# Pieces of 256 columns on GpSimd, both low parts on VectorE, and an earlier square, in an attention and mixture-of-experts kernel

## The chip, the core and the metric

The kernel runs on one core of one Trainium2 chip. The metric is device microseconds of one execution; a smaller number is better. The core's engines are TensorE (PE; its weight loads are a row of their own, PEld), VectorE (DVE), ScalarE (ACT), GpSimd (POOL) and SyncE (SP), which issues most of the transfers.

## What is computed

Three layers in float32. First an attention with pooled keys and values: 8 batches, 8 heads, 576 queries, and the keys and values are means over 8 neighbours. Then each of the 4608 tokens goes to the one of 8 experts that it likes best (512 to 1024 to 512). Then a feed-forward layer (512 to 2048 to 512) with a gated activation.

```python
k_p = k.reshape(B, H, Sp, pool, D).mean(axis=3)     # pool = 8, Sp = 72
v_p = v.reshape(B, H, Sp, pool, D).mean(axis=3)
scores = scale * np.matmul(q, k_p.transpose(0, 1, 3, 2))
attn = softmax(scores);  x = attn @ v_p             # then 4608 tokens of 512
logits = normalised(x) @ normalised(expert_emb).T / tau
expert_idx = np.argmax(logits, axis=1)              # one expert for each token
out[mask] = gate_w[mask, None] * (np.maximum(x[mask] @ w1[e], 0.0) @ w2[e])
h = out @ w_in;  g = h * np.clip(h + 3.0, 0.0, 6.0) / 6.0;  return g @ w_out
```

## The kernel before

**Attention.** The 4608 tokens are walked in 36 tiles of 128. Batch b begins at tile 4.5 b. For each tile PE makes the scores (`emit_S`, L434), VectorE takes their maximum and subtracts it (L442, L445), ScalarE takes the exponential (L449), PE transposes (`emit_T`, L455) and multiplies with the pooled values (`emit_P`, L468), and VectorE divides (L476 to L487), two tiles later than the scores. The order of all instructions is written out by hand, each engine works through its own queue in that order, and small steps of the routing (`emit_route`, `emit_pre`, `emit_gate`, `emit_table`) are woven in one by one by `fill`. GpSimd scatters the token numbers to their experts' lists (`scatter`, L127 and L128).

**Pooling.** A sum over 8 is three rounds of adds that halve: 8 to 4, 4 to 2, 2 to 1. For batches 2 to 7 the values are pooled by GpSimd in `pool_v` (L376, L377, L379: one instruction for each round, over 1536, 768 and 384 columns), and the keys by `pool_k0` (L362, two heads on GpSimd and two on VectorE) and then `pool_k` on GpSimd (L367, 576 columns, and L370). Batches 0 and 1 are pooled in smaller parts by `half_v` (L788 to L790) and `head_k` (L795 to L799), shared between the two engines. The pooled keys `kp` and values have two buffers each, the loaded tiles `k_t`, `v_t`, `q_t` too.

**Start.** ScalarE's queue begins with the store of one row of zeros to `x_dram` (L771; it reads a tile that GpSimd clears first) and then the square of the expert embeddings (L774). The square's sum goes through a chain of VectorE steps (`emit_en`: `emit_sqrt`, then L778 to L782), ten of which stand ahead of `head_k` of batch 0 in VectorE's queue.

**Expert blocks.** The tokens are taken in blocks of 256. A block has four steps j; each has its 512 KB of w1 and of w2. Weights are loaded by GpSimd's indirect DMAs (L157) into four buffers, and `emit_wsplit` splits each into a high part (ScalarE, L169) and a low part (one subtraction over 1024 columns, L170); PE multiplies high with high, high with low and low with high (L262 in `emit_h`, L277 in `emit_y`). The low part of w2 is made by VectorE. That of w1 is made by GpSimd in blocks 0 and 1 (`i < KA - 1`) and by VectorE from block 2 on. Three splits ahead of the blocks (in `prep`, behind the last tiles of the attention) are GpSimd's too. `emit_wload` of the weights four steps ahead stands right behind each split, on GpSimd's queue. In the blocks GpSimd also makes the low parts of w_in (L951).

**Last layer.** From about 720 us on, `emit_h3` and `emit_o` (L1087, L1105) run the feed-forward layer in nine groups of 512 tokens.

Of the kernel before, what the change touches and what calls it, by code (L numbers as in the profile page):

```python
# [8 lines left out]
F32 = mybir.dt.float32  # L9
# [5 lines left out]
ALU = mybir.AluOpType  # L15
# [6 lines left out]
def kernel(  # L22
# [13 lines left out]
    nc = tc.nc  # L36
    NB, P, HP, S = q.shape
# [4 lines left out]
    NT, DM = out.shape  # L42
# [3 lines left out]
    NCH = H * SP // CH  # L46
# [10 lines left out]
    KA = 3  # L57
# [18 lines left out]
    XW = DM + GW  # L76
    x_dram = dram.tile([NT + 1, XW], F32, name="x_dram")
# [73 lines left out]
    def emit_wload(nm, g):  # L151
        i, j = divmod(g, NJ)
        if i >= NBLK or ("load", nm, g) in wdone:
            return
        wdone.add(("load", nm, g))

        nc.gpsimd.indirect_dma_start(  # L157
            out=RAW[nm][j], out_offset=None, in_=WROWS[nm],
            in_offset=bass.IndirectOffsetOnAxis(ap=wrow[:, i, j:j + 1], axis=0),
            bounds_check=NROW - 1, oob_is_err=False)  # L160

    def emit_wsplit(nm, g, eng=nc.vector):
        if g >= NJ * NBLK or ("split", nm, g) in wdone:
            return
        wdone.add(("split", nm, g))
        r = RAW[nm][g % NJ]
        h = SPL[nm + "h"]()
        l = SPL[nm + "l"]()
        nc.scalar.activation(out=h, in_=r, func=AF.Copy)  # L169
        eng.tensor_tensor(out=l, in0=r, in1=h.bitcast(F32), op=ALU.subtract)  # L170
        ws[nm, g] = (h, l)
        emit_wload(nm, g + NJ)

# [32 lines left out]
    def emit_gather(i):  # L206
        if i >= NBLK:
            return
        xg_t[i] = []
        for hf in range(2):  # L210
            xg = XG[hf]()
            nc.gpsimd.indirect_dma_start(
                out=xg, out_offset=None, in_=x_dram[0:NPRE_T, :] if i < KA else x_dram,
                in_offset=bass.IndirectOffsetOnAxis(ap=idx_t[i][:, hf, 0:1], axis=0),
            )
            xg_t[i].append(xg)

    def ahead(i):
        emit_regs(i)
        emit_idx(i)  # L220
# [110 lines left out]
    with ExitStack() as p1:  # L331
# [5 lines left out]
        NKP = 2  # L337
        kps = [one.tile([P, HP, 2, SP], F32, name=f"kp{i}") for i in range(NKP)]
# [25 lines left out]
        def pool_k(b, eng):  # L364
            t = k_t.pop(b)
            kp = kps[b % NKP]
            eng.tensor_tensor(out=t[:, :, 0:2, :], in0=t[:, :, 0:2, :], in1=t[:, :, 2:4, :], op=ALU.add)  # L367
            for s in range(2):
                ps = slice(64 * s, 64 * s + 64)
                eng.tensor_tensor(out=kp[ps, :, s, :], in0=t[ps, :, 0, :], in1=t[ps, :, 1, :], op=ALU.add)  # L370
# [2 lines left out]

        def pool_v(b, eng):
            t = v_t.pop(b)
            eng.tensor_tensor(out=t[:, :, 0:4, :], in0=t[:, :, 0:4, :], in1=t[:, :, 4:8, :], op=ALU.add)  # L376
            eng.tensor_tensor(out=t[:, :, 0:2, :], in0=t[:, :, 0:2, :], in1=t[:, :, 2:4, :], op=ALU.add)  # L377
            vs = wk.tile([CH, NCH, D], F32, name="vs")
            eng.tensor_tensor(out=vs, in0=t[:, :, 0, :], in1=t[:, :, 1, :], op=ALU.add)  # L379
            vs_t[b] = vs  # L380

        def head_of(c):
            return 4 * (c // 3) + c % 3
# [330 lines left out]
        def put(n=1):  # L714
            while pend and n > 0:
                n -= 1
                pend.pop(0)()
# [50 lines left out]
            nc.sync.dma_start(out=idx_dram.rearrange("(p a b) o -> p a (b o)", p=P, b=DR),  # L768
                              in_=dummy.unsqueeze(1).to_broadcast([P, IDXN // P // DR, DR * IW]))

        nc.scalar.dma_start(out=x_dram[NT:NT + 1, :], in_=kps[NKP - 1][0:1].rearrange("p h s c -> p (h s c)")[:, 0:XW])  # L771
        esq = xp.tile([P, DM], F32, name="sq")
        ess = one.tile([E, 1], F32, name="ess")
        nc.scalar.activation(out=esq[0:E], in_=emb_sb, func=AF.Square, accum_out=ess)  # L774

        def emit_en():
            rt = yield from emit_sqrt(ess, [E, 1], "e")
            nc.vector.tensor_scalar(out=rt, in0=rt, scalar1=1e-6, scalar2=tau_sb[0:E], op0=ALU.add, op1=ALU.mult)  # L778
            yield
            nc.vector.reciprocal(out=rt, in_=rt)  # L780
            yield
            nc.vector.tensor_scalar(out=emb_sb, in0=emb_sb, scalar1=rt, scalar2=None, op0=ALU.mult)  # L782
            yield

        def half_v(b, g, eng):

            t, o = v_t[b][:, 3 * g:3 * g + 3], vs_t[b][:, 3 * g:3 * g + 3, :]
            eng.tensor_tensor(out=t[:, :, 0:4, :], in0=t[:, :, 0:4, :], in1=t[:, :, 4:8, :], op=ALU.add)  # L788
            eng.tensor_tensor(out=t[:, :, 0:2, :], in0=t[:, :, 0:2, :], in1=t[:, :, 2:4, :], op=ALU.add)
            eng.tensor_tensor(out=o, in0=t[:, :, 0, :], in1=t[:, :, 1, :], op=ALU.add)  # L790

# [161 lines left out]
    def load_y(u, c0=0, c1=KD):  # L953
        nc.sync.dma_start(out=YL[u % 2][:, c0:c1, :].bitcast(F32), in_=yT_dram[:, c0:c1, 512 * u:512 * u + 512])
# [17 lines left out]
    def flush(q_):  # L972
        while q_:
            for g_ in gens + gates:
                g_[1] = False
            fill(100)
# [7 lines left out]
    def block(i, first):  # L984
        key = CONV[i - 1] if 1 <= i <= len(CONV) else None
        for j in range(NJ):
            g = NJ * i + j
            if i == KA - 2 and j == 2:
                flush(gens)
                flush(gates)  # L990
                put(99)
                ahead(KA)
                ahead(KA + 1)
            if j == 0:
                if i >= KA - 1:
                    ahead(i + 3)
                if i == KA - 1:
                    emit_gather(i + 1)
                if i != KA - 2:
                    emit_gather(i + 2)  # L1000
            if j == 0:
                if i == 0:
                    emit_cload(CONV[0])
                if i + 1 < min(NBLK_MIN + 1, len(CONV) + 3):
                    emit_cload((CONV + outs)[i + 1])
            if i == LOADY:
                load_y(0, j, j + 1)
            if i + j:
                emit_h(i, j)
            more()  # L1010
            if key and j:
                (emit_conv_a, emit_conv_b, emit_conv_c)[j - 1](key)
            if j == 2:
                emit_gated(i + 1)
            if j == 3:
                emit_xT(i + 1)
            emit_wsplit("w1", g + 2, nc.gpsimd if i < KA - 1 else nc.vector)
            more()
            if not (first and j == 0):
                emit_y(*divmod(g - 1, NJ))  # L1020
            more()
            if i == 1 and j == 0:
                late_banks()
            if i == 1 and j == 1:
                PHR.append(PHN[0])
            emit_wsplit("w2", g + 1)
            if i == SPLITY:
                split_y(0, j)
# [162 lines left out]
```

## Time and profile before

| | us |
|---|---|
| median of 3 timed runs | 1502.83 (1501.11 to 1508.79) |
| the profiled execution | 1510.78 |
| its span in the trace | 1509.1 |
| PE busy | 1442.2 (96%) |
| PE weight loads busy | 1291.6 (86%) |
| VectorE busy | 786.9 (52%) |
| ScalarE busy | 625.7 (41%) |
| GpSimd busy | 514.2 (34%) |

All times of rows are of the one profiled execution and are counted from its start. A row of a timeline has the start, the duration, the engine, the line, the operation, the tile written and those read, the shapes, and in brackets the idle time before it and what ended it. "x2" on a row means two instructions one after the other, whose time is given together. The column PEclk is the granted clock of TensorE as a share of full speed (2.4 GHz): 0.50 is the lower level, 1.2 GHz.

### The profile page before, as it was taken

What the parts mean: (1) busy time and instruction counts of PE and PEld (TensorE: products, weight loads), DVE (VectorE), ACT (ScalarE), POOL (GpSimd) and SP (SyncE); (2) the same over time, 40 slices, a digit from 0 to 9 for tenths busy, and PEclk for the clock granted to TensorE, in tenths of its full rate; (3) what the DMA queues carried; (4) which work ended last, traced back from release to release, by engine and by line L of the source; (5) the groups of instructions that cost most, each with busy time, mean ns of one, the idle gap of its engine ahead of it and who ended that gap; (6) DMA issues with size and microseconds to landing.
All of it is one profiled execution on the core that took longest, in us unless ns stands there. A gap on an engine that the chain in (4) does not pass through costs nothing.

```text
span 1509.1 us, 22766 instructions
## 1 busy us (share of the span) xinstructions
PE 1442.2 (96%) x8874; PEld 1291.6 (86%) x8874; DVE 786.9 (52%) x1261; ACT 625.7 (41%) x986; POOL 514.2 (34%) x518
## 2 busy tenths in 40 slices
PE   4997887999999999999999999999999999999997
PEld 4987777999999999999878888888888888888885
DVE  6887747777776777665785322223232322323221
ACT  2663653565565656554443322222222222223221
POOL 6576587755656556554222010010101000010101
PEclk9997998999999999999999999999999999999998
DMA  9875531745742263252321010000101000000000
GB/s 287 289 253 169 156 128 30 245 129 165 242 145 74 58 202 98 59 157 46 127 85 57 0 57 0 29 29 1 56 0 58 1 29 29 27 31 1 28 0 28
DMA packets 88451, 136.15 MB, mean 90 GB/s; under 512 B 43369, under 2 KB 58409, under 8 KB 85874
## 3 DMA queue, kind: packets, MB, share of 16 engines
q1 hardware_dynamic: 45024, 69.10, 14.4%
q0 software_dynamic: 33488, 55.80, 12.2%
q10 hardware_dynamic: 9826, 9.74, 2.0%
q8 instruction: 72, 1.18, 0.3%
q14 instruction: 41, 0.34, 0.1%
HBM read 161.51 MB, written 33.33 MB: 129 GB/s over the span
## 4 chain that ended last, share of the span: by engine, by line
issue 38%; PE 7%; DVE 3%; POOL 2%; ACT 1%; POOLq 0%; ACTq 0%; DVEq 0%
POOL out_dram L128 2%; PE ph L1087 2%; PE psx L1105 2%; PE psz L1105 2%; PE psy L1087 2%; DVE cva L939 1%; DVE rg L1091 1%; DVE cva L941 1%; DVE gl L1094 1%; ACT gh L1093 1%; DVE cva L940 0%; DVE yl L959 0%; POOL apart L127 0%; DVE cva L942 0%; POOL wol L951 0%
## 5 line engine op out<-in xcount | busy, mean ns | idle before, releaser
L157 POOL DMA_INDIRECT rw<-in_w_dram,wrow x179 | 214.1, 1196 | 177.0 <-DVE w1l L170 125.5
L128 POOL DMA_INDIRECT out_dram<-os,idc x36 | 35.1, 975 | 657.7 <-ACT os L1115 651.3
L1091 DVE SCALAR_TENSOR_TENSOR rg<-rg,ph 128x512 f32<-128x512 f32 x72 | 49.6, 689 | 206.3 <-ACT rg L1090 206.3
L1094 DVE TENSOR_TENSOR gl<-rg,gh 128x512 fp32r<-128x512 f32 x144 | 99.8, 693 | 100.7 <-ACT gh L1093 100.0
L1093 ACT ACTIVATE gh<-rg 128x512 fp32r<-128x512 f32 x144 | 91.2, 633 | 145.8 <-DVE rg L1091 141.5
L1091 DVE SCALAR_TENSOR_TENSOR rg<-rg,psy 128x512 f32<-128x512 f32 x72 | 49.5, 687 | 178.5 <-ACT rg L1090 178.5
L1090 ACT ACTIVATE rg<-ph,half 128x512 f32<-128x512 f32 x72 | 49.4, 686 | 208.1 <-PE ph L1087 200.9
L1090 ACT ACTIVATE rg<-psy,half 128x512 f32<-128x512 f32 x72 | 49.4, 686 | 198.7 <-PE psy L1087 198.7
L277 PE MATMUL psy<-hh,w2h 128*128 128x256 f32 x640 | 129.5, 283 | 0.0
L277 PE MATMUL psy<-hl,w2h 128*128 128x256 f32 x640 | 127.6, 281 | 0.0
L277 PE MATMUL psy<-hh,w2l 128*128 128x256 f32 x640 | 127.6, 280 | 0.0
L170 DVE TENSOR_TENSOR w2l<-rw,w2h 128x1024 fp32r<-128x1024 f32 x84 | 110.3, 1313 | 20.8 <-ACT w2h L169 17.6
L170 DVE TENSOR_TENSOR w1l<-rw,w1h 128x1024 fp32r<-128x1024 f32 x76 | 102.7, 1351 | 26.4 <-ACT w1h L169 13.9
L1105 PE MATMUL psx<-wol,gh 128*128 128x512 f32 x288 | 112.4, 390 | 0.4 <-POOL wol L951 0.4
L1105 PE MATMUL psx<-woh,gh 128*128 128x512 f32 x288 | 112.1, 389 | 0.0
L1105 PE MATMUL psx<-woh,gl 128*128 128x512 f32 x288 | 112.0, 389 | 0.0
L1105 PE MATMUL psz<-woh,gh 128*128 128x512 f32 x288 | 112.0, 389 | 0.0
L1105 PE MATMUL psz<-woh,gl 128*128 128x512 f32 x288 | 112.0, 389 | 0.0
L1105 PE MATMUL psz<-wol,gh 128*128 128x512 f32 x288 | 112.0, 389 | 0.0
L265 ACT ACTIVATE hh<-ph 128x512 fp32r<-128x512 f32 x78 | 46.6, 598 | 146.7 <-PE ph L262 131.2
L169 ACT ACTIVATE w2h<-rw 128x1024 fp32r<-128x1024 f32 x85 | 89.9, 1057 | 31.3 <-PE psy L277 20.6
L262 PE MATMUL ph<-xh,w1l 128*128 128x256 f32 x624 | 98.7, 280 | 3.4 <-POOL w1l L170 3.4
(235 smaller groups left out, 3327.5 us busy)
## 6 DMA issues: line engine op xcount, KB each, us to landing
yT_dram<-ys SPq DMA_DIRECT2D x21, 512.0 KB
x_dram<-x ACTq DMA_DIRECT2D x36, 256.0 KB
raw<-in_w_in_dram SPq DMA_DIRECT2D x16, 512.0 KB
raw<-in_w_out_dram SPq DMA_DIRECT2D x16, 512.0 KB
yl<-yT_dram SPq DMA_DIRECT2D x8, 1024.0 KB
k_t<-in_k_dram SPq DMA_DIRECT2D x7, 1152.0 KB
q_t<-in_q_dram SPq DMA_DIRECT2D x7, 1152.0 KB
v_t<-in_v_dram SPq DMA_DIRECT2D x7, 1152.0 KB
```

The lines of the kernel that those rows point to most:

```text
L128: ins = nc.gpsimd.indirect_dma_start(out=dst, out_offset=bass.IndirectOffsetOnAxis(ap=idx, axis=0), in_=src, in_offset=None)
L157: nc.gpsimd.indirect_dma_start(out=RAW[nm][j], out_offset=None, in_=WROWS[nm], in_offset=bass.IndirectOffsetOnAxis(ap=wrow[:, i, j:j + 1], ...
L169: nc.scalar.activation(out=h, in_=r, func=AF.Copy)
L170: eng.tensor_tensor(out=l, in0=r, in1=h.bitcast(F32), op=ALU.subtract)
L262: nc.tensor.matmul(ph[:, f, :], lhsT=a[:, c, fs], rhs=b[:, c, :], start=(n == 0), stop=(n == 3 * KD - 1))
L277: nc.tensor.matmul(o, lhsT=a[:, f, P * c:P * c + P], rhs=b[:, f, :], start=(j == 0 and n == 0 and c % 2 == 0), stop=(j == NJ - 1 and n == ...
L1087: nc.tensor.matmul(ph, lhsT=a[:, c, :], rhs=b[:, c, :], start=(n == 0), stop=(n == 3 * KD - 1))
L1090: nc.scalar.activation(out=r, in_=ph, func=AF.Relu, scale=1.0 / 6.0, bias=half)
L1091: nc.vector.scalar_tensor_tensor(out=r, in0=r, scalar=1.0, in1=ph, op0=ALU.min, op1=ALU.mult)
L1093: nc.scalar.activation(out=gh, in_=r, func=AF.Copy)
L1094: nc.vector.tensor_tensor(out=gl, in0=r, in1=gh.bitcast(F32), op=ALU.subtract)
L1105: nc.tensor.matmul(PO[a], lhsT=x[:, ts], rhs=w, start=(f == 0 and n == 0), stop=(f == NF - 1 and n == 2))
```

## The change

Four edits. (1) In `pool_k`, `pool_v` and the first round of `half_v`, an add is cut along its columns into pieces of 256 (or 288, 192) columns; the same columns are added. (2) In `emit_wsplit`, where GpSimd makes the low part, it does so in four pieces of 256 columns; VectorE still takes 1024 at once. (3) In the blocks 0 and 1, the low part of w1 is no longer given to GpSimd: VectorE makes it, as in the later blocks. (4) ScalarE's queue begins with the square of the embeddings, and the zero row's store follows it. The tile `vs` in `pool_v` is taken ahead of the adds.

```diff
@@ emit_wsplit
-        eng.tensor_tensor(out=l, in0=r, in1=h.bitcast(F32), op=ALU.subtract)
+        n = 256 if eng is nc.gpsimd else 1024
+        for c in range(0, 1024, n):
+            eng.tensor_tensor(out=l[:, c:c + n], in0=r[:, c:c + n], in1=h[:, c:c + n].bitcast(F32), op=ALU.subtract)
@@ pool_k
-            eng.tensor_tensor(out=t[:, :, 0:2, :], in0=t[:, :, 0:2, :], in1=t[:, :, 2:4, :], op=ALU.add)
+            for h in range(0, HP, 2):
+                eng.tensor_tensor(out=t[:, h:h + 2, 0:2, :], in0=t[:, h:h + 2, 0:2, :], in1=t[:, h:h + 2, 2:4, :], op=ALU.add)
@@ pool_v
-            eng.tensor_tensor(out=t[:, :, 0:4, :], in0=t[:, :, 0:4, :], in1=t[:, :, 4:8, :], op=ALU.add)
-            eng.tensor_tensor(out=t[:, :, 0:2, :], in0=t[:, :, 0:2, :], in1=t[:, :, 2:4, :], op=ALU.add)
             vs = wk.tile([CH, NCH, D], F32, name="vs")
-            eng.tensor_tensor(out=vs, in0=t[:, :, 0, :], in1=t[:, :, 1, :], op=ALU.add)
             vs_t[b] = vs
+            for c in range(NCH):
+                eng.tensor_tensor(out=t[:, c, 0:4, :], in0=t[:, c, 0:4, :], in1=t[:, c, 4:8, :], op=ALU.add)
+            for c in range(0, NCH, 2):
+                eng.tensor_tensor(out=t[:, c:c + 2, 0:2, :], in0=t[:, c:c + 2, 0:2, :], in1=t[:, c:c + 2, 2:4, :], op=ALU.add)
+            for c in range(0, NCH, 3):
+                eng.tensor_tensor(out=vs[:, c:c + 3], in0=t[:, c:c + 3, 0, :], in1=t[:, c:c + 3, 1, :], op=ALU.add)
@@ start
-        nc.scalar.dma_start(out=x_dram[NT:NT + 1, :], in_=kps[NKP - 1][0:1].rearrange("p h s c -> p (h s c)")[:, 0:XW])
         nc.scalar.activation(out=esq[0:E], in_=emb_sb, func=AF.Square, accum_out=ess)
+        nc.scalar.dma_start(out=x_dram[NT:NT + 1, :], in_=kps[NKP - 1][0:1].rearrange("p h s c -> p (h s c)")[:, 0:XW])
@@ half_v
-            eng.tensor_tensor(out=t[:, :, 0:4, :], in0=t[:, :, 0:4, :], in1=t[:, :, 4:8, :], op=ALU.add)
+            for c in range(3):
+                eng.tensor_tensor(out=t[:, c, 0:4, :], in0=t[:, c, 0:4, :], in1=t[:, c, 4:8, :], op=ALU.add)
@@ block
-            emit_wsplit("w1", g + 2, nc.gpsimd if i < KA - 1 else nc.vector)
+            emit_wsplit("w1", g + 2)
```

## Rows read from the trace of the kernel before

**Rows 1.** Windows by stage: start:end, length, busy us (instructions), clock, DMA share, GB/s
```profile
core 0: us, PE busy (x) PEld busy (x) DVE busy (x) ACT busy (x) POOL busy (x), PEclk, DMA share, GB/s
0.00:36.00 36.00, 17.05 (x109) 15.28 (x111) 23.78 (x62) 9.77 (x20) 23.53 (x53) 0.96 0.93 283
36.00:110.00 74.00, 69.46 (x581) 65.77 (x579) 62.30 (x158) 45.51 (x101) 51.57 (x50) 0.97 0.82 281
110.00:150.00 40.00, 32.28 (x217) 30.06 (x217) 30.74 (x88) 15.91 (x35) 27.87 (x32) 0.79 0.50 167
193.00:263.00 70.00, 55.10 (x397) 52.17 (x396) 41.05 (x84) 28.42 (x43) 57.09 (x58) 0.90 0.25 75
263.00:1500.00 1237.00, 1232.79 (x7280) 1095.79 (x7280) 597.77 (x756) 499.56 (x732) 328.47 (x299) 1.00 0.23 70
```

**Rows 2.** Timeline of VectorE and of GpSimd, 112 to 123 us
```profile
112.71 3.43 POOL L376 TENSOR_TENSOR v_t<-v_t 96x1536 f32<-96x1536 f32 x1
...
112.74 3.72 DVE L362 TENSOR_TENSOR k_t<-k_t 128x288 f32<-128x288 f32 x1
...
118.20 1.00 POOL L379 TENSOR_TENSOR vs<-v_t 96x384 f32<-96x384 f32 x1
...
118.22 1.04 DVE L537 SCALAR_TENSOR_TENSOR pr<-SH,wgt 128x48 f32<-128x48 f32 x1
...
119.16 0.79 POOL L362 TENSOR_TENSOR k_t<-k_t 128x288 f32<-128x288 f32 x1
...
120.32 0.44 DVE L362 TENSOR_TENSOR k_t<-k_t 128x288 f32<-128x288 f32 x1
```

**Rows 3.** Groups of VectorE's instructions by form, 36 to 193 us
```profile
L362 DVE TENSOR_TENSOR k_t<-k_t 128x288 f32<-128x288 f32 x12 | 15.3, 1272 | 0.0
```

**Rows 4.** Window from 118.6 to 128.8 us
```profile
118.60:128.80 10.20, 10.20 (x53) 9.57 (x52) 5.38 (x17) 5.13 (x15) 7.17 (x10) 0.50 0.77 243
```

**Rows 5.** Line L170, 193 to 720 us: durations min/median/max in ns, and who waited
```profile
L170 DVE TENSOR_TENSOR w1l<-rw,w1h x76: 1209/1226/2900, 269.3 to 708.2; 128x1024 fp32r<-128x1024 f32 x76
L170 POOL TENSOR_TENSOR w1l<-rw,w1h x9: 2348/2377/2421, 193.2 to 265.3; 128x1024 fp32r<-128x1024 f32 x9
...
  PE pm L262: 5.0, 3
...
  PE ph L262: 3.4, 1
```

**Rows 6.** Timeline of VectorE and of GpSimd, 242 to 256 us
```profile
243.88 3.90 DVE L170 TENSOR_TENSOR w2l<-rw,w2h 128x1024 fp32r<-128x1024 f32 x1 [1.51 <-ACT w2h L169]
...
244.34 2.35 POOL L170 TENSOR_TENSOR w1l<-rw,w1h 128x1024 fp32r<-128x1024 f32 x1
```

**Rows 7.** Groups of GpSimd's instructions by form, whole span
```profile
L376 POOL TENSOR_TENSOR v_t<-v_t 96x1536 f32<-96x1536 f32 x6 | 20.7, 3445 | 9.6 <-DMA v_t<-in_v_dram 9.0 <-DVE rd L478 0.3
L377 POOL TENSOR_TENSOR v_t<-v_t 96x768 f32<-96x768 f32 x6 | 11.3, 1888 | 0.5
```

**Rows 8.** Timeline of VectorE and of GpSimd, 61.2 to 64 us
```profile
61.36 1.00 POOL L379 TENSOR_TENSOR vs<-v_t 96x384 f32<-96x384 f32 x1
...
61.63 1.56 DVE L534 TENSOR_TENSOR SH<-LG,m 128x56 f32<-128x56 f32 x1
...
62.33 1.54 POOL L362 TENSOR_TENSOR k_t<-k_t 128x288 f32<-128x288 f32 x2
```

**Rows 9.** Timeline of VectorE and of GpSimd, start to 33 us
```profile
7.88 0.14 DVE L499 TENSOR_SCALAR ess<-ess 8x1 f32<-8x1 f32 x1 [5.26 <-ACT sq L774]
...
14.73 1.80 POOL L788 TENSOR_TENSOR v_t<-v_t 96x768 f32<-96x768 f32 x1 [4.29 <-DMA v_t<-in_v_dram]
...
15.19 1.61 DVE L782 TENSOR_SCALAR emb_sb<-emb_sb,ey 8x512 f32<-8x512 f32 x1
...
30.95 2.26 DVE L799 TENSOR_TENSOR kp<-k_t 64x72 f32<-64x72 f32 x2
```

**Rows 10.** Timelines of GpSimd (85 to 112 us) and of PE (108 to 120 us)
```profile
108.01 0.79 POOL L370 TENSOR_TENSOR kp<-k_t 64x288 f32<-64x288 f32 x1 [1.32 <-DMA idx_dram<-tok,pi]
...
111.28 1.20 PE L434 MATMUL sc<-kp,q_t 128*64 128x144 f32 x16
```

## Prediction

> **What bounds the kernel now.** I read the windows by stage first [rows 1]. From 263 us to the end PE is busy for 1232.79 of 1237.00 us at a granted clock of 1.00: no edit touches PE's work, so this stretch keeps its length and only its beginning can move. Whatever the change is worth lies in the first 263 us. There PE idles 19 of 36 us at the start, 4.5 of 74 between 36 and 110, 7.7 of 40 between 110 and 150, and 14.9 of 70 while the first two expert blocks run, and its mean clock is 0.79 and 0.90 in the last two of these.
>
> Then I looked for what holds VectorE up. The same addition of 288 columns takes 0.44 us at 120.32 and 3.72 us at 112.74 [rows 2]; nothing in its queue differs, but in the second case GpSimd's 1536-column add began 0.03 us before it and ended at 116.14, and VectorE's ended at 116.46, 0.32 us later, about the time its 288 columns need. So a VectorE instruction with two operands in SBUF stands still while a GpSimd add runs, and goes on when that add ends. The twelve instructions of this line take 15.3 us [rows 3], where twelve times 0.44 is 5.3: 10.0 us are waits. VectorE's queue is in order, so the next tile's maximum waits too, and PE behind it. Afterwards PE runs at the lower clock level: 10.20 us of work with a granted 0.50, that is 1.2 GHz, right after the wait of 112.74 [rows 4].
>
> In the expert blocks GpSimd's low part of w1 is late as well as in the way: PE waits 5.0 + 3.4 = 8.4 us for it [rows 5], and VectorE's low part of w2, 1.22 us by itself, takes 3.90 us when one of them runs [rows 6].
>
> **The change part by part.**
>
> *Price of the pieces.* The instructions of 1536 and 768 columns take 3.445 and 1.888 us [rows 7]: 2.03 ns a column and 0.33 us beside. Two of 288 columns one behind the other take 1.54 us [rows 8], 0.77 each, so a piece of 256 in a run costs about 0.77 - 32 x 0.00203 = 0.70. Six make 4.2 us for 3.445, three make 2.1 for 1.888, and the third round and `pool_k` gain about 0.1 each: some 1.2 us more of GpSimd for each of six batches. No stage is bound by GpSimd throughout (51.57 us busy of 74 [rows 1]); what hides the extra is its idle time, and what it costs if that cover is gone is the second rival.
>
> *Does a waiting VectorE instruction get in between two pieces?* This decides the attention. Rows 2 have a yes: at 118.22 VectorE's 48-column step is held by the GpSimd add of 118.20, which ends at 119.20; GpSimd's next begins at 119.16 with no gap, and VectorE's step ends at 119.26, so it went in between. Rows 8 have both answers: VectorE's step of 61.63 is passed over at 62.36, where the next add follows at 62.33, and gets in about 62.33 + 0.77 = 63.10 (it ends at 63.19). The two cases differ in who asked first: at 118.22 VectorE asked 0.02 us after GpSimd's add began, at 61.63 0.27 us after it; and there the add uses 96 partitions and the next one 128. The pieces of `pool_v` all use 96. I take it that VectorE gets in at the next boundary, or at the second: a wait of at most 0.7, seldom 1.4 us, where it was up to 3.3.
>
> The row shows that GpSimd begins an instruction before the last has ended. The Trainium skill has a rule that speaks against this change (GPSIMD Engine Reference, Instruction dispatch): consecutive Pool instructions are no barrier, a core starts the next as soon as its own share is done. By that, a run of pieces could hold VectorE off as one long instruction; the first rival is what it would give here. By the row of 118.22 it need not.
>
> *Start (edit 4).* VectorE's embedding chain begins at 7.88 after waiting 5.26 us for ScalarE's square [rows 9], which stands behind a store that waits for GpSimd. Moved ahead, it can come up to 5.26 us earlier and not later; the keys of batch 0 must have landed too. I take 3, near the middle. The last step of the chain, L782, takes 1.61 us because GpSimd's L788 holds it (14.73 to 16.53); 3 us earlier it is through before. The two key steps at 30.95 take 2.26 us behind GpSimd's pooling, whose values land at a time that the transfers set (DMA share 0.93 [rows 1]), so an earlier VectorE passes ahead of it. That is 3 + 1 + 2 = 6, less 1 for VectorE's own `half_v`, now three pieces that may meet GpSimd's: 5 us, bounds 2 and 7. The store that now comes second on ScalarE's queue has nothing urgent behind it.
>
> *36 to 110 us.* The pieces save VectorE some microseconds, but PE is busy for 69.46 of 74: the gain is between 0 and 4.5; I take 1.5, since PE's idle time is what is left between dependent tiles.
>
> *110 to 150 us.* At a mean clock of 0.79, 42% of the 40 us ran at 0.50, nearly 17 us, with some 15 us of PE work, of which half, 7.5, comes back at full clock. PE then needs 32.28 - 7.5 = 24.8 us; at the density of the stretch before (69.46/74) that is 26.4 us, a gain of 13.6. VectorE needs 30.74 less the 3.28 + 0.82 of rows 2, 26.6 us; at its density (62.30/74) 31.6 us, a gain of 8.4. I take 9, nearer to VectorE's. The bounds are 0, if the clock falls anyway, and 13.6.
>
> *Expert blocks (edits 2 and 3).* GpSimd loses 8 x 2.377 = 19.0 us of 57.09, VectorE gains 8 x 1.226 = 9.8 us on 41.05 of 70 [rows 1, 5]. The 8.4 us for which PE waited go. PE ran about 20% of these 70 us at 0.50, 14 us, and has lost 6 or 7 by it; I give back 3. New is that VectorE waits for ScalarE's high part of w1; queued behind it are the low part of w2, of the hidden layer and of the next tokens, for which PE waits, and on GpSimd the next weight load. From block 2 on it has always been so, with PE at 1232.79 of 1237.00 us, so I charge 1.5 us, for the routing's last steps, which share VectorE here alone. Sum 10, bounds 5 and 14. The three splits that stay on GpSimd cost 0.4 us each more, ahead of the blocks.
>
> *Sum.* 5 + 1.5 + 9 + 10 = 25.5 us; the waits between 150 and 193 us I leave out. The profiled execution took 1510.78 us (span 1509.1): 1485.3. The median of the timed runs lies 8 us lower, at 1502.83, and they differ among themselves by 7.7. Since only the first 263 us have waits of this size, I assume that the difference is such meetings of the two engines, which the change removes in part: half of the 8 us, then, is in my sum already. 1485.3 - 4 = 1481.
>
> **The rivals.**
>
> *The pieces hold VectorE off as one.* Then a run lasts 4.2 + 2.1 + 1.1 = 7.4 us plus the key adds of 0.8 behind it, where single adds with a gap let VectorE in after 3.43. The wait of 112.74 would last until about 120.9 + 0.3, 8.5 us for 3.72, and its like comes once in each of the six batches: 6 x 4.8 = 29 us, of which 4 replace later waits that these already contain. Against it stand 10 us of the blocks and 3 of the start: 25 - 13 = 12 us slower, 1515. It decides for slower from 2.2 us of additional wait in a batch (13/6). For it: 62.36 in rows 8. Against it: 118.22 in rows 2.
>
> *GpSimd becomes the late one in the attention.* The keys of batch 5 are ready at 108.80 and PE's scores need them at 111.28 [rows 10]: a margin of 2.5 us, while GpSimd gets 1.2 us longer in a batch. If it stays where it is, 36 to 150 us give nothing: 5 + 10 = 15 us, 1502.8 - 15 = 1488. Against it: most of GpSimd's waits are for transfers and for VectorE, which come earlier too.
>
> *VectorE becomes the late one in the blocks.* Its 41.05 us contain waits of the kind of rows 6, but if the low part of w1 stands behind the table's steps, the blocks give nothing: 25.5 - 10 = 15.5, 1510.8 - 15.5 - 4 = 1491.
>
> *Both of these,* or the pieces change when VectorE waits but not how long: 5 us of the start remain, 1498.
>
> **How the numbers follow.** Forecast (both gains) 0.55, GpSimd late 0.15, VectorE late 0.10, both 0.10, held off 0.10. The predicted time is the forecast's, 1481. Its own bounds are 7 + 4.5 + 13.6 + 14 = 39 us, which gives 1510.8 - 39 - 4 = 1468, and 2 + 0 + 0 + 5 = 7. The range reaches from 1467 over the rivals to 1500, without the first of them. About 0.5%, 7.5 us, is what a measurement of this kernel can tell from no change: faster 0.55 + 0.15 + 0.10 = 0.80, same 0.10, slower 0.10.
>
> **What would show it.** The additions of 288 columns on VectorE should take 1.2 us at most in the attention; if some take 5 to 8 us, the first rival holds. The window from 110 to 150 us should show no stretch at 0.50 and its work should end some 15 us earlier. PE should wait for no low part of w1. VectorE's L499 should begin near 5 us. The time from the first tokens of block 2 to the end, 1240 us or so, must be the same; if it moves, the forecast rests on the wrong stage. It would be wrong if the clock falls in other places, or if the transfers of keys and values, which fill 0.82 of the DMA time up to 110 us, set the pace once VectorE doesn't.

## The result, and the profile after

The changed kernel takes 1478.93 us (median of 4 runs, 1476.68 to 1480.31) where the kernel before took 1504.66 in the same comparison: a ratio of 0.9824 with a 95% interval of 0.9805 to 0.9843. That is 1.8% faster, 26.5 us by this ratio and 25.7 by the two medians. 1481 was forecast. The profiled execution took 1476.68 us with a span of 1475.0. It lies 34.1 us under the profiled execution of before, which was itself some 6 us slower than its kernel's median; the traces therefore show more than the medians do.

The windows by stage of the kernel after (the columns are those of [rows 1]). The cuts follow the same stages, but not to the tile, so clocks and shares can be set beside [rows 1], lengths can't:

```profile
core 0: us, PE busy (x) PEld busy (x) DVE busy (x) ACT busy (x) POOL busy (x), PEclk, DMA share, GB/s
0.00:36.00 36.00, 21.58 (x156) 19.05 (x157) 25.19 (x75) 13.72 (x27) 24.56 (x59) 1.00 0.93 289
36.00:98.50 62.50, 57.16 (x479) 54.37 (x478) 45.37 (x131) 38.02 (x89) 48.44 (x72) 0.95 0.90 309
98.50:133.00 34.50, 30.27 (x240) 28.20 (x241) 28.42 (x87) 17.86 (x38) 32.23 (x52) 0.95 0.64 208
133.00:177.50 44.50, 41.63 (x329) 38.74 (x328) 36.61 (x134) 28.78 (x63) 29.86 (x43) 0.92 0.53 160
177.50:243.00 65.50, 62.36 (x509) 60.74 (x508) 50.08 (x102) 36.59 (x53) 54.81 (x64) 0.97 0.40 114
243.00:1475.00 1232.00, 1219.43 (x7170) 1083.54 (x7168) 585.94 (x746) 491.29 (x721) 322.14 (x294) 1.00 0.23 69
```

Blocks 0 and 1 alone, from the first tokens of block 0 to the first of block 2, hold the same 390 matmuls in both kernels. Before, and after:

```profile
189.56:257.10 67.54, 52.59 (x391) 49.73 (x389) 36.85 (x87) 26.93 (x41) 55.96 (x60) 0.92 0.27 79
```

```profile
174.02:223.88 49.86, 47.68 (x390) 46.58 (x388) 35.24 (x93) 26.84 (x41) 42.34 (x54) 0.97 0.38 116
```

PE's idle time in them has gone from 15.0 of 67.5 us to 2.2 of 49.9, and the mean clock from 0.92 to 0.97. Between 98.5 and 177.5 us it is 0.95 and 0.92, where it was 0.79 between 110 and 150. The first stage is as full of transfers as before (0.93), and the second is fuller (0.90).

Two marks in the trace divide the gain: the first matmul of h in block 0 (it ends the attention) and the first matmul of the last layer. The first comes at 178.09 instead of 193.63 us, 15.5 earlier; from there to the second it takes 501.77 us instead of 520.59, 18.8 less. What follows the second mark is the same within 0.3 us.

The place of [rows 2] in the kernel after, in the timelines of VectorE and of GpSimd:

```profile
110.66 4.37 POOL L383 TENSOR_TENSOR v_t<-v_t 96x256 f32<-96x256 f32 x6
...
110.91 0.54 DVE L541 TENSOR_TENSOR SH<-LG,m 128x48 f32<-128x48 f32 x1
...
111.48 0.65 DVE L544 SCALAR_TENSOR_TENSOR pr<-SH,wgt 128x48 f32<-128x48 f32 x1
...
112.90 0.61 DVE L550 TENSOR_TENSOR oh<-pr,pm 128x48 bf16<-128x48 f32 x1
...
113.61 0.83 DVE L364 TENSOR_TENSOR k_t<-k_t 128x288 f32<-128x288 f32 x1
```

Six pieces run without a gap for 4.37 us, and four of VectorE's steps with two operands in SBUF end inside that run. Each is held, the addition of 288 columns for 0.39 us (0.83 against 0.44 alone), but none for longer than a piece. The groups by form say the same of all batches, and give the price of a piece:

```profile
L364 DVE TENSOR_TENSOR k_t<-k_t 128x288 f32<-128x288 f32 x12 | 6.9, 574 | 4.3 <-DMA k_t<-in_k_dram 4.3
...
L383 POOL TENSOR_TENSOR v_t<-v_t 96x256 f32<-96x256 f32 x36 | 25.8, 746 | 9.6 <-DMA v_t<-in_v_dram 9.2
```

Twelve additions take 6.9 us, where [rows 3] had 15.3. A piece of 256 takes 0.75 us in the mean (0.70 was the estimate).

PE's waits in the blocks of the kernel after (us in total, times, longest), where [rows 5] had 8.4 us for w1's low part:

```profile
PE pm L264 <- ACT xh L250: 1.3, 2, 0.9
PE ph L264 <- DVE xl L251: 0.9, 1, 0.9
PE psx L246 <- ACT xg L236: 0.8, 2, 0.7
```

At the start VectorE's chain begins at 3.23 us instead of 7.88, and the first maximum is taken 4.3 us earlier. But this lead doesn't last, as VectorE's and then PE's timeline show:

```profile
3.23 0.14 DVE L506 TENSOR_SCALAR ess<-ess 8x1 f32<-8x1 f32 x1 [0.61 <-ACT sq L780]
...
51.55 0.46 DVE L364 TENSOR_TENSOR k_t<-k_t 128x288 f32<-128x288 f32 x1 [3.81 <-DMA k_t<-in_k_dram]
```

```profile
53.64 2.26 PE L441 MATMUL sc<-kp,q_t 128*128 128x144 f32 x8 [4.20 <-issue]
```

VectorE, now early, waits 3.81 us for the keys of batch 3, PE stands idle for 4.20 us, and in this idle time its clock falls to the lower level, 1.2 GHz, for 6.7 us (a granted 0.50 from 51.4 to 58.1).

### The profile page after: what moved, and what is told of

Its sections match the earlier page's. It is cut to its first block, busy times and chain, and to the rows that moved or that the text cites. A ratio compares the mean times of both kernels' runs of the same rounds, so it can differ in the third digit from the quotient of the medians.

```text
span 1475.0 us, 22840 instructions
## 1 busy us (share of the span) xinstructions
PE 1432.4 (97%) x8874; PEld 1284.6 (87%) x8874; DVE 771.6 (52%) x1271; ACT 626.3 (42%) x986; POOL 512.0 (35%) x579
## 4 chain that ended last, share of the span: by engine, by line
issue 39%; PE 12%; POOL 2%; POOLq 0%; ACT 0%
PE ph L1095 3%; PE psx L1113 3%; PE psy L1095 3%; PE psz L1113 3%; POOL out_dram L128 2%; POOL apart L127 0%; POOLq L1195 0%; POOLq L128 0%; ACT os L1123 0%
## 5 line engine op out<-in xcount | busy, mean ns | idle before, releaser
L172 DVE TENSOR_TENSOR w1l<-rw,w1h 128x1024 fp32r<-128x1024 f32 x84 | 111.9, 1332 | 30.2 <-ACT w1h L169 28.1
L172 DVE TENSOR_TENSOR w2l<-rw,w2h 128x1024 fp32r<-128x1024 f32 x84 | 103.8, 1236 | 13.4 <-ACT w2h L169 11.7
L169 ACT ACTIVATE w2h<-rw 128x1024 fp32r<-128x1024 f32 x85 | 89.9, 1058 | 29.7 <-PE psy L279 20.1
L264 PE MATMUL ph<-xl,w1h 128*128 128x256 f32 x624 | 99.2, 280 | 1.1 <-DVE xl L251 0.9
```

The lines of the kernel that those rows point to most:

```text
L172: eng.tensor_tensor(out=l[:, c:c + n], in0=r[:, c:c + n], in1=h[:, c:c + n].bitcast(F32), op=ALU.subtract)
L264: nc.tensor.matmul(ph[:, f, :], lhsT=a[:, c, fs], rhs=b[:, c, :], start=(n == 0), stop=(n == 3 * KD - 1))
```

## The experiments

The theories. *As forecast:* the parts are worth 5 (square), 10.5 (pieces) and 10 us (VectorE makes w1's low part) and add up. *From the two traces:* the start's lead is taken back by transfers, and the blocks are worth nearly twice as much, since GpSimd's queue and not only one product in it is late there.

The table has all kernels. The gain is (1 - ratio) x 1505 us, uncertain by about 3 us each (6 for e_w1v, 4 for a few others). "First h" and "blocks" are the two marks, from one profiled execution each: when block 0's first h begins, and the time from there to the last layer.

| kernel | ratio to before, 95% interval | gain us | first h | blocks |
|---|---|---|---|---|
| before | 1 | 0 | 193.63 | 520.59 |
| changed | 0.9824 [0.9805, 0.9843] | 26.5 | 178.09 | 501.77 |
| e_pieces | 0.9973 [0.9952, 0.9994] | 4.1 | 178.08 | 523.84 |
| e_w1v | 0.9873 [0.9833, 0.9913] | 19.1 | 189.23 | 500.52 |
| e_sq | 0.9989 [0.9966, 1.0012] | 1.7 | 183.65 | 522.75 |
| a_w1pool | 0.9988 [0.9965, 1.0012] | 1.8 | 177.99 | 527.53 |
| a_iota | 0.9989 [0.9972, 1.0005] | 1.7 | 174.61 | 521.88 |
| a_nosq | 0.9823 [0.9800, 0.9846] | 26.6 | 180.82 | 500.54 |
| a_v1536 | 0.9866 [0.9843, 0.9890] | 20.2 | 191.54 | 500.90 |
| a_fill6 | 0.9811 [0.9784, 0.9839] | 28.4 | 180.16 | 501.15 |
| a_iota5 | 0.9923 [0.9904, 0.9942] | 11.6 | 184.69 | 510.13 |
| a_v512 | 0.9917 [0.9892, 0.9942] | 12.5 | 182.29 | 515.56 |
| a_v512_again | 0.9918 [0.9888, 0.9947] | 12.3 | 184.97 | 516.26 |
| a_prepv | 0.9918 [0.9896, 0.9941] | 12.3 | 195.97 | 513.96 |

The kernel before and e_w1v have the same attention, and their first h stand 4.4 us apart: so much does one execution's attention differ from another's. The blocks are steadier: the five kernels with the changed blocks up to a_fill6 lie between 500.5 and 501.8.

### Each part alone

**e_pieces.** 

> The kernel before with edit 1 alone: GpSimd pools in pieces of 256 columns, and splits the three weights ahead of the blocks in pieces; in the blocks GpSimd still makes the low part of w1 in one instruction of 1024 columns. The forecast's terms for this edit are 1.5 us (36 to 110) and 9 us (110 to 150): 10 us faster than before, some 1494 us at a median of before of 1504.7, with the first h of block 0 some 10 us earlier than 193.6 and the time from there to the first h3 unchanged at 520.6 us. The theory that the transfers set the pace up to 57 us and that the pieces clear the way behind it says the same sum with another place: nothing before 57 us, 8 to 12 us between 110 and 178. The rival that the runs of pieces hold VectorE off as one says slower than before, 1510 or more.

```diff
 # the kernel before, with pool_k, pool_v and half_v as in the change, and
-        eng.tensor_tensor(out=l, in0=r, in1=h.bitcast(F32), op=ALU.subtract)
+        n = 256 if eng is nc.gpsimd and g < 2 else 1024
+        for c in range(0, 1024, n):
+            eng.tensor_tensor(out=l[:, c:c + n], ...)
```

Measured: 1502.29 us against 1505.93, 4 us faster. The attention ends at 178.08, as early as in the changed kernel, but the blocks take 523.84 us, 3.3 more than in the kernel before. Its window over blocks 0 and 1, GpSimd's groups in it and PE's waits:

```profile
173.44:246.12 72.68, 56.09 (x391) 53.91 (x390) 42.08 (x89) 28.17 (x42) 60.68 (x68) 0.84 0.28 82
```

```profile
L157 POOL DMA_INDIRECT rw<-in_w_dram,wrow x18 | 20.9, 1163 | 5.2 <-POOL w1l L172 1.9 <-issue 1.8 <-DVE rw L515 0.3
L172 POOL TENSOR_TENSOR w1l<-rw,w1h 128x1024 fp32r<-128x1024 f32 (+1 forms) x10 | 17.0, 1713 | 0.1
L128 POOL DMA_INDIRECT idx_dram<-tok,pi x16 | 16.4, 1023 | 3.5 <-issue 3.0 <-POOL apart L127 0.3 <-DVE x L491 0.2
```

```profile
PE pm L264 <- POOL w1l L172: 10.1, 3, 6.0
PE ph L264 <- POOL w1l L172: 4.5, 1, 4.5
```

GpSimd is busy for 60.68 of 72.68 us; the idle time before its instructions is the 0.2 to 0.3 us ahead of each indirect DMA (5.2 us for 18, 3.5 for 16). So its queue has no gap for two whole blocks: weight loads, index stores and w1's low part stand one behind the other, and PE waits 14.6 us for the last of them. An earlier attention only lets PE arrive earlier at this queue. The Trainium skill (Perfetto Trace Analysis, DMA Instruction — SWDGE (GPSIMD)) says that the profile's end of a DMA issued by GpSimd is the end of writing its descriptors there, not of the transfer; the trace agrees: weight loads are listed here with 1.16 us in the mean, and land 2.5 us after their issue (the median).

**e_w1v.** 

> The kernel before with the edit of the blocks alone: VectorE makes the low part of w1 in blocks 0 and 1. The forecast's term is 10 us (5 to 14): 1495 us, first h unchanged at 193.6, and the 520.6 us from the first h to the first h3 become 510. The theory from the trace after, that this stretch holds 18 to 19 us which all hang on this edit, says 502 us for the stretch and 1486 us. The rival that half of the gain in the blocks came with the pieces (the three splits ahead of the blocks, and a GpSimd queue that is emptier when the blocks begin) says 511 and 1495 too, and then e_pieces must show the other half in its own stretch from the first h to the first h3.

```diff
-            emit_wsplit("w1", g + 2, nc.gpsimd if i < KA - 1 else nc.vector)
+            emit_wsplit("w1", g + 2)
```

Measured: 1486.71 us, 19.1 us faster, and blocks of 500.52 us. This one line is nearly three quarters of the whole change. GpSimd loses 8 x 2.377 = 19.0 us of work [rows 5], and the stretch becomes 20.1 us shorter. The rival that half of this came with the pieces falls: e_pieces has none of it.

**e_sq.** 

> The kernel before with the square moved ahead of the zero row's store alone. The forecast's term is 5 us (2 to 7): 1499.7 us, with the first maximum 4 to 5 us earlier than 16.7. The theory that transfers set the pace up to 57 us says that the first maximum is 4 us earlier but that the lead is gone at tile 9 or so: 0 to 2 us in the end, 1503 to 1504.7. The rival that nothing is given back says 4 us or more, 1500 or less.

Measured: 1504.74 against 1505.93, a gain of 1.7 us that can't be told from none. Its first maximum comes at 12.60 us instead of 16.73, its eleventh at 64.29 instead of 65.53: of a lead of 4.1 us, 1.2 are left there.

**a_w1pool**, the opposite of e_w1v, on the changed kernel. 

> The changed kernel, with GpSimd making the low part of w1 in blocks 0 and 1 again, now in four pieces of 256 columns (2.8 us together instead of 2.38). If what counted in the blocks is that GpSimd delivers w1 late, nearly the whole term comes back: PE waits 8 us or more for it, the stretch from the first h to the first h3 is 515 us or more instead of 501.8, and the time is 1490 to 1498 us. If what counted is that GpSimd holds VectorE up, the pieces cure that as in the attention: no wait of VectorE above 0.8 us for them, a stretch of 505 us or less and 1482 us or less.

```diff
-            emit_wsplit("w1", g + 2)
+            emit_wsplit("w1", g + 2, nc.gpsimd if i < KA - 1 else nc.vector)
```

Measured: 1503.72 us; 24.7 of the 26.5 us are gone. So pieces don't cure the blocks. VectorE is held for 0.6 us at most in blocks 0 and 1; what counts is PE's waits there:

```profile
PE pm L264 <- POOL w1l L172: 9.8, 8, 4.3
PE ph L264 <- POOL w1l L172: 2.3, 4, 1.3
```

### Is it the one product, or the whole queue?

Both e_pieces and a_w1pool leave it open whether PE suffers because w1's low part itself stands in GpSimd's queue, or because anything there makes all the rest late. So GpSimd got work that nobody waits for.

**a_iota.** 

> The changed kernel with work for GpSimd added that nobody reads: ten index fills of 128x80 (0.22 to 0.24 us each, 2.4 together, as long as the low part of w1 was) in each of the 8 groups of blocks 0 and 1, 19 us in all. The theory that GpSimd's queue as a whole sets the pace of blocks 0 and 1 (weight loads, index stores and gathers stand in it one behind the other with no gap) says that most of the 19 us come back: 1494 to 1504 us, blocks 0 and 1 each 6 us longer or more. The rival that only the low part of w1 was urgent in this queue, since PE waits for it in the same group, and that all else there has a block of slack, says 1479 to 1484 us and no PE wait above 1 us in these blocks.

```diff
             emit_wsplit("w1", g + 2)
+            if i < KA - 1:
+                for _ in range(10):
+                    nc.gpsimd.iota(scr, pattern=[[P, 5], [0, 16]], base=0, channel_multiplier=1)
```

Measured: 1503.86 us. With VectorE making the product as in the changed kernel, the blocks take 521.88 us, 20.1 more than there and as long as before the change. The time as a whole is 24.8 us longer. The other 5 us lie in the last layer, where the fills are long over: there the same 3456 matmuls take longer (the windows from the second mark on, of the changed kernel and of this one). a_iota5 below has this too, no other kernel has, and its cause isn't known.

```profile
679.80:1475.00 795.20, 785.09 (x3456) 649.60 (x3456) 276.36 (x398) 230.51 (x369) 58.72 (x88) 0.99 0.10 33
```

```profile
696.50:1497.00 800.50, 790.00 (x3456) 649.05 (x3456) 276.51 (x398) 230.53 (x369) 58.39 (x88) 1.00 0.10 32
```

GpSimd's timeline and PE's and ScalarE's waits in the first blocks:

```profile
236.62 2.65 POOL L1029 IOTA scr<- 128x80 int32 x10
239.91 1.12 POOL L158 DMA_INDIRECT rw<-in_w_dram,wrow  x1 [0.63 <-issue]
241.34 1.00 POOL L158 DMA_INDIRECT rw<-in_w_dram,wrow  x1 [0.30 <-issue]
242.35 2.64 POOL L1029 IOTA scr<- 128x80 int32 x10
```

```profile
PE psx L247 <- ACT xg L237: 19.1, 3, 11.1
```

```profile
ACT w2h L170 <- DMA rw<-in_w_dram,wrow: 18.0, 4, 6.0
ACT xg L237 <- DMA xg<-x_dram,idx: 15.3, 2, 14.5
```

PE doesn't wait for GpSimd at all by these rows. It waits 19.1 us for ScalarE, which waits 15.3 for gathered tokens and 18.0 for weights, whose transfers GpSimd issued late. Most of it shows only in block 2. Block 0 takes no longer than in the changed kernel and block 1 6 us longer, where 6 or more were expected for each; block 2 takes 14 us longer. There stands the gather of the tokens of block 3, behind all eight runs of fills: in the changed kernel it begins 63.4 us after the first h, here 85.5 (the timelines of GpSimd, of the changed kernel and of this one):

```profile
241.47 1.21 POOL L214 DMA_INDIRECT xg<-x_dram,idx  x1 [0.30 <-PE psy L279]
```

```profile
260.07 0.96 POOL L215 DMA_INDIRECT xg<-x_dram,idx  x1 [0.30 <-DMA raw<-in_w_in_dram]
```

So the queue as a whole sets the pace. The added work is 8 runs of 2.65 us, 21.2 us; the stretch grew by 20.1.

**a_iota5**, half of it. 

> The changed kernel with five instead of ten of the unread index fills in each of the 8 groups of blocks 0 and 1: 40 x 0.20 = 8 us of GpSimd instead of 16.4, which cost 25 us (1503.9 against 1478.9). If GpSimd's queue sets the pace of these blocks in the changed kernel too, with nothing to spare, every us counts from the first: about half of the 25, 1488 to 1494 us. If the changed kernel has slack there and the ten fills went past it, most of the 8 us vanish: 1479 to 1483 us, PE waits below 2 us in these blocks.

Measured: 1499.55 us; the blocks take 510.13 us. Seven runs of five fills took 1.31 us each and the last 1.58, 10.7 us in all, and the stretch grew by 8.4. (Its total also holds the 5.6 us more of the last layer, and comes from another chip, see a_v512 below. The stretch comes from its own trace.) Put together, work of GpSimd in blocks 0 and 1 against the length of the stretch:

| kernel | GpSimd's extra work, us | blocks, us |
|---|---|---|
| e_w1v, changed | 0 | 500.5, 501.8 |
| a_iota5 | 7 x 1.31 + 1.58 = 10.7 | 510.1 |
| before, e_sq, e_pieces | 8 x 2.38 = 19.0 | 520.6, 522.8, 523.8 |
| a_iota | 8 x 2.65 = 21.2 | 521.9 |
| a_w1pool | 32 pieces x 0.85 = 27.2 | 527.5 |

(28 pieces of w1 took 22.9 us in a_w1pool, 0.85 each: some of them are held by VectorE.) Nearly every microsecond on this queue is one of the kernel's, whoever needs the result. The changed kernel has hardly any to spare there: from 174 to 256 us no gap in its GpSimd's work is longer than 0.31 us.

### The attention: which edit, and where the start's lead goes

**a_v1536.** 

> The changed kernel with whole instructions in the pooling of the values (1536, 768 and 384 columns), all other pieces as changed. With the low part of w1 off GpSimd's queue, the edits of the attention together are worth 1486.7 - 1478.9 = 7.8 us. The theory that it is VectorE's waits behind the long adds says that nearly all of it is here: 1484 to 1488 us, additions of 288 columns of up to 3.7 us, and a stretch at half the clock between 110 and 150 us. The rival that the start and the pieces of the keys bring it says 1479 to 1482.

```diff
-            for c in range(NCH):
-                eng.tensor_tensor(out=t[:, c, 0:4, :], in0=t[:, c, 0:4, :], in1=t[:, c, 4:8, :], op=ALU.add)
...
+            eng.tensor_tensor(out=t[:, :, 0:4, :], in0=t[:, :, 0:4, :], in1=t[:, :, 4:8, :], op=ALU.add)
...
```

Measured: 1486.29 us, so the pieces of the values are worth 6.3 us (uncertain by some 4); e_w1v against the changed kernel gives 7.4 for all that isn't the blocks. Two stretches of 6.8 us at half the clock, from 128.5 and from 142.1 us, came back with the long adds, as expected. Its longest wait is not an addition of 288 columns (2.0 us at most, where 3.7 were expected) but a routing step, in the timelines of VectorE and of GpSimd:

```profile
139.11 3.49 DVE L662 SCALAR_TENSOR_TENSOR pcw<-pc,pcm,wgt 128x8 f32<-128x8 f32 x1
```

```profile
139.16 3.42 POOL L379 TENSOR_TENSOR v_t<-v_t 96x1536 f32<-96x1536 f32 x1
```

A step of 0.17 us takes 3.49, to the end of the long add. The Trainium skill (SBUF — State Buffer, Who interferes with whom) says that a VectorE instruction with two inputs in SBUF contends with a GpSimd instruction that reads it, for a pair of ports that is an exclusive lock. By that rule small steps suffer as much as large ones; the trace agrees, with 3.49 us here. A piece bounds the wait, though not always to one piece: in the changed kernel a single wait between 20 and 178 us is longer than 0.7 us. It is a step of 0.15 us that takes 1.05, in the timelines of VectorE and of GpSimd:

```profile
134.80 1.05 DVE L684 TENSOR_TENSOR pcw<-pcu 128x8 f32<-128x8 f32 x1
```

```profile
134.69 1.14 POOL L387 TENSOR_TENSOR vs<-v_t 96x192 f32<-96x192 f32 x2
```

It asks while the first of two pieces of 192 columns runs, is passed over between them, and ends at 135.85, when both have (a_fill6 below has a longer case).

**a_nosq.** 

> The changed kernel with the zero row's store ahead of the square again (edit 4 undone). The forecast's term for it is 5 us (2 to 7): 1484 us. The theory that the transfers up to 57 us take the lead of the start back says 0 to 2 us: 1479 to 1481, with the first maximum some 4 us later than 12.5 and the maximum of tile 9 within 1.5 us of 55.9.

```diff
-        nc.scalar.activation(out=esq[0:E], in_=emb_sb, func=AF.Square, accum_out=ess)
         nc.scalar.dma_start(out=x_dram[NT:NT + 1, :], ...)
+        nc.scalar.activation(out=esq[0:E], in_=emb_sb, func=AF.Square, accum_out=ess)
```

Measured: 1478.40 us against 1478.93: nothing. The first maximum and that of tile 10 in VectorE's timeline, of the changed kernel and then of this one:

```profile
12.46 0.74 DVE L449 TENSOR_REDUCE mx<-sc 128x8 f32<-128x576 f32 x1
...
62.56 0.74 DVE L449 TENSOR_REDUCE mx<-sc 128x8 f32<-128x576 f32 x1
```

```profile
15.77 0.74 DVE L449 TENSOR_REDUCE mx<-sc 128x8 f32<-128x576 f32 x1
...
63.25 0.74 DVE L449 TENSOR_REDUCE mx<-sc 128x8 f32<-128x576 f32 x1
```

Edit 4 puts the first maximum 3.3 us earlier and the eleventh 0.7. The lead is gone by 63 us: in between lie the waits for the keys of batch 3 and for its values (9.2 us of GpSimd's, the row of L383 above), and PE's stretch at the lower clock. (The maximum of tile 9, 55.94 and 58.93, stood 3 us apart still, which is more than expected.)

**a_fill6.** 

> The changed kernel with the 2.4 MB fill of the index table issued at tile 6, behind the loads of batch 3, and no longer at tile 3, ahead of them. In the changed kernel VectorE waits 3.81 us for the keys of batch 3 at 51.55, PE is idle for 4.20 us behind it and then runs 6.8 us at half the clock. The theory that the transfers set the pace there because this fill stands ahead of them says that these waits go: 3 to 6 us, 1473 to 1476 us. The rival that the fill costs the DMA engines the same 8 us wherever it stands, and holds up the keys of batch 4 in place of those of batch 3, says 1478 to 1480.

```diff
-        at(3, fill_idx)
+        at(6, fill_idx)
```

Measured: 1477.12 us (1471.91 to 1482.23), 1.9 us better than the changed kernel by the ratios and not to be told from it. The time of 1473 to 1476 us that the theory expected isn't reached. The wait is gone as it expected: the eight additions of 288 columns up to 98 us wait 1.9 us for keys instead of 4.3, none at batch 3. But the first h comes at 180.16, no earlier than in the changed kernel, and up to there PE is at the lower clock for 17.1 us in both traces, here mostly from 138.6 on (10.2 us). So the fill did hold the keys up, and taking it away doesn't show in the end; what takes its place after 60 us isn't settled.

This trace has the longest wait of any kernel with the pieces of 256, in the timelines of VectorE and of GpSimd:

```profile
59.06 2.21 DVE L544 SCALAR_TENSOR_TENSOR pr<-SH,wgt 128x56 f32<-128x56 f32 x1
```

```profile
58.16 1.54 POOL L364 TENSOR_TENSOR k_t<-k_t 128x288 f32<-128x288 f32 x2
59.66 1.53 POOL L370 TENSOR_TENSOR k_t<-k_t 128x288 f32<-128x288 f32 x2
61.27 1.64 POOL L373 TENSOR_TENSOR kp<-k_t 64x288 f32<-64x288 f32 x2
```

The step, 0.22 us by itself, asks at 59.06, while the second add of 58.16 runs. It is passed over at 59.66 and again in the middle of the next row, and ends at 61.27, in the one gap of this run (61.19 to 61.27).

### What stays open: the size of the pieces, and two chips

**a_v512.** 

> The changed kernel with the value pooling in pieces of 512, 384 and 192 columns instead of 256, 256 and 192. The theory that VectorE waits for the end of the piece that runs, and gets in at that boundary, says waits of up to 512 x 0.00203 + 0.2 = 1.2 us instead of 0.7, some 0.5 us in one or two places of each batch, against 0.5 us less of GpSimd in a batch: 1477 to 1481 us, no addition of 288 columns above 1.8 us. The rival that a piece twice as long is worth half of the whole edit lost says 1482 or 1483.

```diff
-            for c in range(NCH):
-                eng.tensor_tensor(out=t[:, c, 0:4, :], ...)
+            for c in range(0, NCH, 2):
+                eng.tensor_tensor(out=t[:, c:c + 2, 0:4, :], ...)
```

**a_prepv.** 

> The changed kernel with VectorE making the low parts of w2 of group 0 and of w1 of group 1, so that GpSimd has 2 x 2.8 us less directly ahead of block 0 and in it. If GpSimd's queue still sets the pace of blocks 0 and 1, this gives 3 to 6 us: 1473 to 1476. If it has slack there, or VectorE is as late (2 x 1.23 us more among the routing's steps), it gives nothing: 1478 to 1481.

**a_v512_again.** 

> The kernel of a_v512 once more, beside the kernel before. On the chip of that call the kernel before took 1510.28 us, 5 us more than elsewhere, and three quite different kernels all came to ratios of 0.992; the changed kernel itself was not among them. If that chip (or its state) was the cause, the pieces of 512 give what the changed kernel gives, a ratio of 0.980 to 0.984 (some 1477 to 1481 us where before takes 1504.7), and the stretch from the first h to the first h3 is 500 to 502 us as in the changed kernel. If the size of the pieces is the cause, the ratio is again near 0.992 and that stretch again 510 us or more.

Measured: 1496.52, 1500.58 and 1498.22 us, ratios of 0.992 in all three, as for a_iota5. The kernel before took 1510.28 us on the chip of the first two (and of a_iota5) and 1509.30 on that of the last, 5 us more than on the others (1504.57 to 1505.93). The changed kernel was not run beside any of these three. The attention agrees with the theory of one piece: VectorE's longest wait up to 178 us is 1.03 us, in a routing step of 0.17 us,

```profile
130.62 1.19 DVE L513 TENSOR_TENSOR rw<-ry 128x20 f32<-128x20 f32 x1
```

and the first h comes at 182.29, against 184.69 for a_iota5, which has the 256-column pieces, on the same chip. The loss lies in blocks 0 and 1, whose code is the changed kernel's (the stretch takes 515.56 and 516.26 us; counted from the first h, block 2 begins 12 to 14 us later than in the changed kernel, in a_prepv too). There PE runs at a granted 0.50 (1.2 GHz) for a long time, with idle time between its matmuls most of which the profile puts down to nothing. The window in a_v512_again:

```profile
203.20:220.20 17.00, 11.24 (x41) 9.23 (x42) 3.62 (x7) 4.77 (x6) 8.91 (x15) 0.50 0.03 4
```

In blocks 0 and 1 PE is at this level for 13.7 us in a_v512, 13.7 in a_prepv and 17.1 in a_v512_again; in the five other kernels with these blocks it is 3.4 us at most. a_iota5 has none in blocks 0 and 1, on the same chip as the first two. Its gain of 11.6 us is also what is left of 26.5 without its own losses, 8.4 us in the blocks and 5.6 in the last layer (12.5): that chip takes nothing from it that shows. This speaks against the chips as the only cause, and a_v512_again came out as expected if the size of the pieces is it. But its chip too is one on which the kernel before is slow, and a_prepv, which has the pieces of 256, lost as much. Whether the chips or the edits do it, by way of what VectorE and GpSimd do when block 0 begins, isn't settled. Nor is it settled whether a_prepv's own edit takes or gives anything: its blocks lose 12 us, but its attention also ended late, at 195.97.

## Why the prediction was right, and where it was not

The time was right, the direction too, and the mechanism of the pieces was. The sizes of the parts were not: one term too small and two too large made up for each other, and that the sum came out within 3 us is luck.

- **Price of a piece, and the wait for it.** Right: 0.75 us for an estimate of 0.70. VectorE gets in at the next boundary as a rule: in the changed kernel's trace one wait after 20 us is above 0.7, the 0.9 at 134.80. "Seldom 1.4" was right too: in seven other traces with these pieces, each with some 25 to 30 held steps, eight waits are of 1.0 to 2.0 us (e_pieces, a_nosq and a_prepv one each, a_w1pool two, a_fill6 three). So the first rival's mechanism exists, a step can be passed over for several pieces, but nothing in the attention takes the 5 to 8 us that it needed.
- **Start, 5 us.** Wrong in the end, right at its place. The first maximum is 4.3 us earlier; a_nosq shows that the edit is worth 0 with the rest in place, and e_sq can't be told from 0 alone. The step that failed is that a lead at the start was carried through to the end. The prediction had named its condition last (transfers that fill 0.82 of the DMA time up to 110 us), and gave it no price.
- **36 to 150 us, 10.5 us.** Too much. All edits of the attention together give 7.4 us with the blocks relieved, 6.3 by a_v1536 for the values, and 4.1 alone. The expected 15 us by the end of the attention are there in the profiled executions (15.5), but these differ by 4 us with the same code, and the profiled execution of before took 6 us more than the median: the traces show some 8 us more than the ratio does, and nearly all of it here, since the blocks agree (18.8 and 19.1). For these 6 us the sum has 4. The forecast that no stretch at 0.50 would be left between 110 and 150 failed: three of about 3.4 us are, from 116.2, 133.2 and 140.1.
- **Expert blocks, 10 us with bounds of 5 and 14.** Mis-sized: e_w1v measured 19.1 (a_w1pool, the same edit taken out, 24.7). The term was built from PE's named waits, 8.4 us, and a guess for its clock. What bounded these blocks was GpSimd, and its row was in the prediction: busy for 57.09 of 70 us [rows 1], with 33 indirect DMAs that each have 0.2 to 0.3 us ahead of them which don't count as busy. The 19.0 us that the edit takes off this queue were written down, and used only as a relief; they were the gain. PE's wait for one product was the symptom that the profile named.
- **The sum.** It took the parts as independent. They aren't: while GpSimd makes w1's low part, the pieces and the square move the attention's end by up to 15 us in the traces and the time by 1.8 us (a_w1pool), since the queue of the next stage takes the lead.
- **The other rivals.** VectorE late in the blocks: refuted, PE's waits for VectorE there are 0.9 us. GpSimd late in the attention: PE waits for it once between 32 and 178 us, for 1.8 us at a piece of the values, far from the 10.5 us at stake. **From block 2 on nothing changes:** right, 1252.0 us from its first tokens to the end before and 1251.1 after.

## What to carry to other kernels

Before pricing a stage by the bottleneck engine's named waits, add up the in-order queue of every engine that feeds it, with the fixed time ahead of each of its DMAs: an engine without a gap sets the pace even where only one of its results is seen to be late, and what is taken off it comes back one for one. Test this with work that nobody reads, and read the stage's own length beside the total: here the added work also came with 5 us in a stage that it doesn't touch. A lead won ahead of a stage that is bound by another engine or by transfers is worth little until that bound is moved (0 to 4 us here), so edits are to be priced in the order of those bounds and not one by one.

## What the hardware showed

- A run of GpSimd pieces lets VectorE in at most boundaries, but not at all of them: waits up to 0.7 us with 256 columns as a rule, 1.0 with 512, 3.3 with 1536, for steps that need 0.17 us as for long ones. Where a step is passed over it waits 0.9 to 1.5 us, and once 2.0 over three pieces of 288, to the next gap.
- Work on GpSimd that nobody reads costs as much as work that is waited for: 10.7 and 21.2 us of index fills made the blocks 8.4 and 20.1 us longer, the second mostly one block later, by the gather that stood behind them.
- In the two kernels with these fills the 3456 matmuls of the last layer take 790 us, in all others 784 to 786; the cause isn't known.
- Ten index fills of 128x80 took 2.65 us together though each is listed with 0.20: some 0.06 us lie between two of them.
- In three kernels, on two chips, 14 to 17 us at the lower clock appeared in blocks whose code runs in others with 3.4 us of it at most; for most of the idle time in it no row names what PE waits for.
